# First channel product of a spectral mixer by Strassen's scheme, with its sums on VectorE

## The chip, the cores and the metric

The kernel runs on one core of one Trainium2 chip. The core has TensorE (PE in the profile; PEld is its weight load), VectorE (DVE), ScalarE (ACT), GpSimd (POOL) and the queue engine SP, each working through its own instructions in order, tied together by semaphores. The metric is the device time of one execution in microseconds (us); lower is better.

## The reference

```
X = rfft(x, axis=1)                                  # x: 8 x 3008 x 256
Yr = Xr @ w_r - Xi @ w_i + b_r ; Yi = Xr @ w_i + Xi @ w_r + b_i
Y = softshrink(Yr, 0.01) + 1j * softshrink(Yi, 0.01)
x = irfft(Y, n=3008, axis=1)                         # 8 x 3008 x 256
h = relu(x^T @ w_tok1) @ w_tok2                      # mixes the 3008 tokens
u = x + h^T
out = u + relu(u @ w_ch1) @ w_ch2                    # w_ch1: 256 x 1536, w_ch2: 1536 x 256
```

The last line is the channel stage, and it is the largest piece of work. `u @ w_ch1` is the first channel product; `relu(...) @ w_ch2` is the second.

## The kernel before

The 8 batches are handled in five units: `UNITS` is [0], [1], [2,3], [4,5], [6,7]. For each unit a spectral part (the `spectral` generator: Fourier transforms as matmuls, the complex product in `mix`, the inverse, and the token sums) comes first, and a channel part (`channel`) follows. The channel part of unit u and the spectral part of unit u+1 are interleaved by hand: at each `yield` of `channel` the main loop lets the spectral generator issue as many of its steps as a pace in `left_s` and `left_c` allows. The last unit's channel part has no spectral work beside it. From this program order the tile framework makes each engine's final order and adds the waits; each engine then runs its list strictly in that order.

Every product that feeds the output is made more precise by splitting both sides into a high and a low part in the type float32r: `mm3` issues three matmuls (high by high, high by low, low by high, L175 to L177) into one sum in PSUM.

The channel part walks over token chunks of up to 512 columns. A chunk of `u` (256 channels as 2 tiles of 128 rows) is made by `make_u` and split into `uh` and `ul` by `split_u`. There are 12 tiles of 128 hidden features. For each tile f:

- `first(f)`: 2 channel tiles by 3 passes, so 6 matmuls over the chunk's columns, into a PSUM bank `ph`.
- ACT writes `hh`, the rectified high part (L746), and DVE writes `hlo`, the rest (L747), both reading `ph`.
- `second(f)`: 6 matmuls of `hh` and `hlo` against `w2h` and `w2l` into `po`. It is issued two tiles later than `first(f)`, so that ACT and DVE have two tiles' time.

In the spectral part, `forward` makes `px` on PE, ACT copies it to `xf`, POOL adds its third plane (L424), and ACT and DVE split it into `xth` and `xtl`, which are the stationary sides of the 18 matmuls `pm` of `mix`. These tiles have two buffers, and `mix` of a step stands behind `forward` of the step after it. `tokens` adds all its products up in PSUM, in two banks `gp` that are held for the whole unit.

PSUM has 8 banks: 4 go round as `bank(...)`, two hold `po`, two hold `gp`.

## Time and profile before

| | |
|---|---|
| median of 3 runs | 2456.27 us (2453.36 to 2458.68) |
| the profiled execution | 2458.71 us, of which the span from the first to the last instruction is 2456.7 us |
| PE busy | 2423.6 us (99%), 12748 matmuls |
| PEld (weight loads, beside PE) | 2108.6 us (86%) |
| DVE busy | 1107.5 us (45%) |
| ACT busy | 873.3 us (36%) |
| POOL busy | 305.1 us (12%) |
| mean granted TensorE clock | 0.996 |

A matmul's duration in the profile covers its way through the array, and matmuls overlap: what one costs the queue is the distance from its start to the next one's start, called its pitch here. Idle time of an engine is put down to what ended it.

### The profile page before, as it was taken

What the parts mean: (1) busy time and instruction counts of PE and PEld (TensorE: products, weight loads), DVE (VectorE), ACT (ScalarE), POOL (GpSimd) and SP (SyncE); (2) the same over time, 40 slices, a digit from 0 to 9 for tenths busy, and PEclk for the clock granted to TensorE, in tenths of its full rate; (3) what the DMA queues carried; (4) which work ended last, traced back from release to release, by engine and by line L of the source; (5) the groups of instructions that cost most, each with busy time, mean ns of one, the idle gap of its engine ahead of it and who ended that gap; (6) DMA issues with size and microseconds to landing.
All of it is one profiled execution on the core that took longest, in us unless ns stands there. A gap on an engine that the chain in (4) does not pass through costs nothing.

```text
span 2456.7 us, 31566 instructions
## 1 busy us (share of the span) xinstructions
PE 2423.6 (99%) x12748; PEld 2108.6 (86%) x12748; DVE 1107.5 (45%) x1773; ACT 873.3 (36%) x1583; POOL 305.1 (12%) x259
## 2 busy tenths in 40 slices
PE   6999999999999999999999999999999999999999
PEld 5878999988888888888888898888888888888887
DVE  6975665454544444434344354434334333232332
ACT  4764444443334343333333343333333222222222
POOL 0000222222222111111111111111111000000000
PEclk8999999999999999999999999999999999999999
DMA  9775334552233462222222263222321112112110
GB/s 269 238 244 152 95 112 141 156 174 90 84 98 111 114 179 84 65 72 88 89 76 69 94 176 105 80 87 80 101 66 38 63 56 63 49 58 80 37 55 18
DMA packets 148946, 252.15 MB, mean 103 GB/s; under 512 B 11009, under 2 KB 101089, under 8 KB 148801
## 3 DMA queue, kind: packets, MB, share of 16 engines
q1 hardware_dynamic: 122289, 199.80, 27.2%
q10 hardware_dynamic: 26512, 50.34, 6.5%
q8 instruction: 100, 1.64, 0.3%
q14 instruction: 45, 0.37, 0.0%
HBM read 162.68 MB, written 87.43 MB: 102 GB/s over the span
## 4 chain that ended last, share of the span: by engine, by line
PE 93%; DMA 4%; DVE 1%; ACT 1%; SPq 0%; issue 0%; POOL 0%; DVEq 0%; ACTq 0%
PE ph L175 10%; PE ph L176 10%; PE po L175 10%; PE po L177 10%; PE po L176 10%; PE ph L177 10%; PE pu L708 4%; PE px L421 3%; PE pm L177 2%; PE pm L175 2%; PE pm L176 2%; PE pu L175 2%; PE pu L176 2%; PE pu L177 2%; PE gp L175 2%; PE gp L177 2%
## 5 line engine op out<-in xcount | busy, mean ns | idle before, releaser
L747 DVE SCALAR_TENSOR_TENSOR hlo<-ph,hh 128x512 fp32r<-128x512 f32 (+4 forms) x588 | 391.6, 667 | 646.0 <-ACT hh L746 643.0
L746 ACT ACTIVATE hh<-ph 128x512 fp32r<-128x512 f32 (+4 forms) x588 | 340.5, 580 | 815.8 <-PE ph L177 812.9
L175 PE MATMUL ph<-uh,w 128*128 128x512 f32 (+4 forms) x1176 | 456.0, 388 | 0.4 <-DVE hlo L747 0.3
L176 PE MATMUL ph<-ul,w 128*128 128x512 f32 (+4 forms) x1176 | 449.6, 382 | 0.3 <-DVE ul L717 0.3
L177 PE MATMUL ph<-uh,w 128*128 128x512 f32 (+4 forms) x1176 | 448.8, 382 | 0.0
L175 PE MATMUL po<-hh,w2h 128*128 128x512 f32 (+4 forms) x1176 | 448.7, 382 | 0.0
L176 PE MATMUL po<-hlo,w2h 128*128 128x512 f32 (+4 forms) x1176 | 448.1, 381 | 0.0
L177 PE MATMUL po<-hh,w2l 128*128 128x512 f32 (+4 forms) x1176 | 448.0, 381 | 0.0
L177 PEld LDWEIGHTS ph<-uh,w 128*128 128x128 f32 x1176 | 221.1, 188 | 39.4
L175 PEld LDWEIGHTS po<-hh,w2h 128*128 128x128 f32 x1176 | 221.1, 188 | 38.7
L176 PEld LDWEIGHTS po<-hlo,w2h 128*128 128x128 f32 x1176 | 221.0, 188 | 38.7 <-DVE hlo L747 0.2
L177 PEld LDWEIGHTS po<-hh,w2l 128*128 128x128 f32 x1176 | 220.9, 188 | 38.4
L175 PEld LDWEIGHTS ph<-uh,w 128*128 128x128 f32 x1176 | 221.5, 188 | 35.8 <-DVE hlo L747 1.4
L176 PEld LDWEIGHTS ph<-ul,w 128*128 128x128 f32 x1176 | 221.6, 188 | 34.6 <-DVE ul L717 0.7
L137 DVE TENSOR_TENSOR xtl<-xf,xth 128x768 fp32r<-128x768 f32 x84 | 80.5, 958 | 193.7 <-ACT xth L134 193.5
L715 ACT COPY uf<-pu 128x470 f32<-128x470 f32 (+23 forms) x188 | 62.6, 375 | 233.0 <-PE pu L708 233.0
L175 PE MATMUL pm<-wmh,xth 128*128 128x256 f32 x504 | 144.5, 287 | 0.1
L137 POOL TENSOR_TENSOR yl<-z,yh 128x512 fp32r<-128x512 f32 x72 | 92.7, 1288 | 413.2 <-ACT yh L134 413.2
L177 PE MATMUL pm<-wmh,xtl 128*128 128x256 f32 x504 | 142.5, 283 | 0.4 <-DVE xtl L137 0.3
L176 PE MATMUL pm<-wml,xth 128*128 128x256 f32 x504 | 142.4, 283 | 0.0
L708 PEld LDWEIGHTS pu<-g,b 96*128 96x128 f32 x1024 | 130.8, 191 | 3.4
L424 POOL TENSOR_TENSOR xf<-xf 128x256 f32<-128x256 f32 x84 | 69.7, 830 | 499.8 <-ACT xf L423 499.4
(124 smaller groups left out, 3213.5 us busy)
## 6 DMA issues: line engine op xcount, KB each, us to landing
wt<-wt_d SPq DMA_DIRECT2D x28, 940.0 KB, 5.5
x<-in_x SPq DMA_DIRECT2D x39, 480.0 KB, 4.3
a<-a_d SPq DMA_DIRECT2D x36, 512.0 KB, 3.9
b_d<-bt ACTq DMA_DIRECT2D x36, 512.0 KB, 3.3
out<-o SPq DMA_DIRECT2D x34, 512.0 KB, 2.8
a_d<-a ACTq DMA_DIRECT2D x36, 480.0 KB, 3.3
wt<-wt_d SPq DMA_DIRECT2D x21, 752.0 KB, 5.1
b<-b_d SPq DMA_DIRECT2D x32, 480.0 KB, 6.2
```

The lines of the kernel that those rows point to most:

```text
L137: lo_eng.tensor_tensor(out=lo, in0=src, in1=hi.bitcast(F32), op=ALU.subtract)
L175: PE.matmul(out, lhsT=wh, rhs=xh, start=start, stop=False)
L176: PE.matmul(out, lhsT=wh, rhs=xl, start=False, stop=False)
L177: PE.matmul(out, lhsT=wl, rhs=xh, start=False, stop=stop)
L421: PE.matmul(pt[:, o:o + 128], lhsT=x, rhs=f2cols(2 * kp + ab), start=True, stop=True)
L424: (V if plain else G).tensor_tensor(out=xf[:, 0], in0=xf[:, 1], in1=xf[:, 2], op=ALU.add)
L708: PE.matmul(pt[:, s * TOKS:(s + 1) * TOKS], lhsT=b2[:, s, cs], rhs=g2[:, 0 if s0 + s == 0 else 1], start=False, stop=s == k - 1)
L715: S.copy(out=ufs[m][:, ct, lo - at:hi - at], in_=pt[:, lo - c0:hi - c0])
L746: S.activation(out=hh, in_=pt, func=AF.Relu)
L747: V.scalar_tensor_tensor(out=hlo, in0=pt, scalar=0.0, in1=hh.bitcast(F32), op0=ALU.max, op1=ALU.subtract)
```

## The change

The first channel product is regrouped. A chunk's columns are cut into two halves of h = cw/2, the 256 channels into two tiles (already so), and the 12 feature tiles into 6 pairs. Per pair this is a 2 by 2 by 2 block product, which Strassen's scheme (in Winograd's form) makes with 7 block products in place of 8:

- `split_w1` makes from `w_ch1` four sums of blocks per pair (DVE) and stores 7 blocks, each split into high and low.
- `split_u(n, part)` makes four sums of blocks of the chunk (DVE) and splits 7 blocks `b11, b21, t1, t3, t2, t4, b22` (ACT high, DVE low). In the built program these are tiles named `u2_...` (two blocks each) and `u1_...` (`b22`).
- `pair(p)` makes the 7 products, each as 3 matmuls over h columns, into three PSUM banks `s1, s2, s3` (named `ph`), and adds them up: one copy on ACT (`cu`), three additions of h columns and two of cw columns on DVE.
- `features` takes such a sum of cw columns, written by DVE to SBUF (`hf`), rectifies it twice on ACT (once into `hh`, once in place), and subtracts on POOL: `hlo = hf - hh`. Before, ACT rectified once out of PSUM and DVE made `hlo` out of PSUM. The feature tile that comes from `s3` is called t1 in `pair`, the one from `s2` t0.
- `second` no longer issues its 6 matmuls; it puts them in a list `todo`, and `fill(k)` issues k of them at four places of the next pair.

`tokens` adds up in SBUF (`ga`): two matmul groups per step go to a bank and DVE adds them. The two PSUM banks so freed make the round 6 banks long. `hh` and `hlo` have 2 buffers in place of 3. The spectral tiles `xf, xth, xtl, wt, et` have one buffer in place of two, the output tile `o` has one in place of three, the loads of `w_d` and `e` go one step ahead in place of two, and `mix` of a step now stands ahead of `forward` of the next one. The chunks are cut anew: 48 (33 of 512 columns, 14 of 480, one of 448) in place of 49.

```diff
-    ps = ctx.enter_context(tc.tile_pool(name="ps", bufs=4, space=bass.MemoryType.PSUM))
+    ps = ctx.enter_context(tc.tile_pool(name="ps", bufs=6, space=bass.MemoryType.PSUM))
...
-        wt = wk.tile([128, 2, 2, DT], F32R, name="wt")
+        wt = wk.tile([128, 2, 2, DT], F32R, name="wt", bufs=1)
         split(wt[:, 0], wt[:, 1], wf, S, eng)
         return wt
 
     def split_e(ef, eng):
-        et = wk.tile([128, 2, 2, 128], F32R, name="et")
+        et = wk.tile([128, 2, 2, 128], F32R, name="et", bufs=1)
         split(et[:, 0], et[:, 1], ef, S, eng)
...
-    def split_w1(q, t, f):
-        cols = slice(q * 512, (q + 1) * 512)
-        split(wc["w1"][:, 0][:, t, cols], wc["w1"][:, 1][:, t, cols], f, S, V)
+    def split_w1(q, ws):
+        v0, v1 = (w.rearrange("p (r f c) -> p r f c", r=2, f=2) for w in ws)
+        sm = wk.tile([128, 4, 2, 128], F32, tag="o", name="ws", bufs=1)
+        V.tensor_tensor(out=sm[:, 0], in0=v0[:, :, 1], in1=v1[:, :, 1], op=ALU.add)
+        V.tensor_tensor(out=sm[:, 1], in0=sm[:, 0], in1=v0[:, :, 0], op=ALU.subtract)
+        V.tensor_tensor(out=sm[:, 2], in0=v0[:, :, 0], in1=v0[:, :, 1], op=ALU.subtract)
+        V.tensor_tensor(out=sm[:, 3], in0=v1[:, :, 0], in1=sm[:, 1], op=ALU.subtract)
+        d = wc["w1"][:, 2 * q:2 * q + 2]
+        split(d[:, :, 0, 0], d[:, :, 0, 1], v0[:, :, 0], S, V)
+        split(d[:, :, 1:3, 0], d[:, :, 1:3, 1], v1, S, V)
+        for k in range(4):
+            split(d[:, :, 3 + k, 0], d[:, :, 3 + k, 1], sm[:, k], S, V)
...
-            xh = wk.tile([128, 3, 2, 128], F32R, name="xth", bufs=2)
-            xl = wk.tile([128, 3, 2, 128], F32R, name="xtl", bufs=2)
+            xh = wk.tile([128, 3, 2, 128], F32R, name="xth", bufs=1)
+            xl = wk.tile([128, 3, 2, 128], F32R, name="xtl", bufs=1)
...
             if kp == 0:
-                acc.append(ps1.tile([128, 2, 512], F32, name="gp"))
-            gp = acc[0]
-            for i in range(2):
-                for jt in range(2):
-                    js = slice(jt * 128, (jt + 1) * 128)
-                    start, stop = kp == 0 and i == 0, kp == KP - 1 and i == 1
+                acc.append(ps1.tile([128, 2, 512], F32, tag="po", name="gp") if plain else wc["wk2"].tile([128, 2, 512], F32, name="ga", bufs=1))
+            ga = acc[0]
+            for jt in range(2):
+                js = slice(jt * 128, (jt + 1) * 128)
+                pt = ga[:, jt] if plain else bank("gp")
+                for i in range(2):
                     if plain:
-                        PE.matmul(gp[:, jt, :w], lhsT=wt[:, i, js], rhs=y[:, i], start=start, stop=stop)
+                        PE.matmul(pt[:, :w], lhsT=wt[:, i, js], rhs=y[:, i], start=kp == 0 and i == 0, stop=kp == KP - 1 and i == 1)
                     else:
-                        mm3(gp[:, jt, :w], wt[:, 0, i, js], wt[:, 1, i, js], rows(y, 0, i), rows(y, 1, i), start, stop)
+                        mm3(pt[:, :w], wt[:, 0, i, js], wt[:, 1, i, js], rows(y, 0, i), rows(y, 1, i), i == 0, i == 1)
+                if not plain:
+                    if kp == 0:
+                        V.tensor_copy(out=ga[:, jt, :w], in_=pt[:, :w])
+                    else:
+                        V.tensor_tensor(out=ga[:, jt, :w], in0=pt[:, :w], in1=ga[:, jt, :w], op=ALU.add)
...
-        for kp in range(2):
-            ws[kp] = load_w(w_d, kp), load_e(kp)
+        ws[0] = load_w(w_d, 0), load_e(0)
         lag = 4 if nb == 1 else 3
         for n in range(len(steps) + lag):
-            if n < len(steps):
-                kp, b = steps[n]
-                if b == 0 and kp + 1 < KP:
-                    a2s[kp + 1] = p.load_a(kp + 1)
-                xts[n] = p.forward(kp, b, a2s[kp])
-                yield 0.9
             m = n - 1
             if 0 <= m < len(steps):
                 kp, b = steps[m]
@@ -524,6 +531,12 @@
                         ys[kp] = hl([128, 2, 2, C], "yh"), hl([128, 2, 2, C], "yl")
                 p.mix(xts.pop(m), ys[kp][0][:, :, b], ys[kp][1][:, :, b])
                 yield 2.15
+            if n < len(steps):
+                kp, b = steps[n]
+                if b == 0 and kp + 1 < KP:
+                    a2s[kp + 1] = p.load_a(kp + 1)
+                xts[n] = p.forward(kp, b, a2s[kp])
+                yield 0.9
...
-            wc["w1"] = const.tile([128, 2, 2, DF], F32R, tag="w1", name="w1")
...
-        widths = [k * TOKS for k in sizes] if u == 0 else [total % CW] + [CW] * (total // CW)
+        short = -total % CW
+        widths = [CW - short] + [CW] * (total // CW) if u == 0 else [480] * (short // 32) + [CW] * ((total + short) // CW - short // 32)
...
+    def split_u(n, part):
+        h = chunks[n][2] // 2
+        if part == 0:
+            uf = ufs.pop(n)
+            sm = t4([128, 2, 2, CW // 2], "us")
+            us[n] = uf, {}, sm
+        uf, blocks, sm = us[n]
+        sums, more = sm[:, 0, :, :h], sm[:, 1, :, :h]
+        def block(names, src):
+            t = wc["wk2"].tile([128, 2, len(names), CW // 2], F32R, name=f"u{len(names)}", bufs={1: 1, 2: 4}[len(names)])
+            split(t[:, 0, :, :h], t[:, 1, :, :h], src, S, V)
+            for i, k in enumerate(names):
+                blocks[k] = t[:, 0, i, :h], t[:, 1, i, :h]
+        if part == 0:
+            V.tensor_tensor(out=sums, in0=uf[:, :, h:2 * h], in1=uf[:, 0, :2 * h].rearrange("p (i c) -> p i c", i=2), op=ALU.subtract)
+            V.tensor_tensor(out=more[:, 0], in0=uf[:, 1, h:2 * h], in1=sums[:, 0], op=ALU.subtract)
+            V.tensor_tensor(out=more[:, 1], in0=uf[:, 1, :h], in1=more[:, 0], op=ALU.subtract)
+            block(("b11", "b21"), uf[:, :, :h])
+        else:
+            block(("t1", "t3"), sums)
+            block(("t2", "t4"), more)
+            block(("b22",), uf[:, 1:, h:2 * h])
+    todo = []
+    def fill(k):
+        for _ in range(min(k, len(todo))):
+            todo.pop(0)()
     def channel(n):
         u, at, cw = chunks[n]
...
+        h = cw // 2
+        uf, blocks, _ = us.pop(n)
         after = chunks[n + 1] if n + 1 < len(chunks) else None
...
+        po = []
+        def product(out, p, a, b):
+            hi, lo = blocks[b]
+            mm3(out, wc["w1"][:, p, a, 0], wc["w1"][:, p, a, 1], hi, lo, True, True)
+        def add(out, x, y):
+            V.tensor_tensor(out=out, in0=x, in1=y, op=ALU.add)
+        def features(x, y):
+            hh, hlo, raw = (wc["wk2"].tile([128, CW], t, name=k)[:, :cw] for k, t in (("hh", F32R), ("hlo", F32R), ("hf", F32)))
+            add(raw.rearrange("p (i c) -> p i c", i=2), x, y)
+            S.activation(out=hh, in_=raw, func=AF.Relu)
+            S.activation(out=raw, in_=raw, func=AF.Relu)
+            G.tensor_tensor(out=hlo, in0=raw, in1=hh.bitcast(F32), op=ALU.subtract)
+            return hh, hlo
+        def second(f, t, first, last):
+            hh, hlo = t
+            w = (wc["w2h"], hh), (wc["w2h"], hlo), (wc["w2l"], hh)
             for ct in range(2):
...
+                for i, (m, x) in enumerate(w):
+                    def one(ct=ct, i=i, m=m, x=x):
+                        if first and ct == 0 and i == 0:
+                            po.append(ps1.tile([128, 2, 512], F32, tag="po", name="po"))
+                        PE.matmul(po[0][:, ct, :cw], lhsT=m[:, f, ct * 128:(ct + 1) * 128], rhs=x, start=first and i == 0, stop=last and i == 2)
+                    todo.append(one)
+            if last:
+                todo.append(store)
...
+        def halves(name):
+            return bank(name).rearrange("p (i c) -> p i c", i=2)[:, :, :h]
+        def pair(p):
+            s1, s2, s3 = (halves("ph") for _ in range(3))
+            u = wc["wk2"].tile([128, 2, CW // 2], F32, name="cu")[:, :, :h]
+            u3 = wc["wk2"].tile([128, CW // 2], F32, name="c3")[:, :h]
+            product(s1[:, 0], p, 0, "b11")
+            S.copy(out=u[:, 0], in_=s1[:, 0])
+            product(s1[:, 1], p, 4, "t2")
+            add(u[:, 1], s1[:, 1], u[:, 0])
+            fill(3)
+            yield 1.4
+            product(s2[:, 0], p, 1, "b21")
+            product(s1[:, 0], p, 5, "t3")
+            add(u3, s1[:, 0], u[:, 1])
+            fill(3)
+            yield 1.4
+            product(s3[:, 0], p, 2, "t4")
+            product(s3[:, 1], p, 3, "t1")
+            t1 = features(s3, u3.rearrange("p (o c) -> p o c", o=1).to_broadcast([128, 2, h]))
+            add(u[:, 1], s3[:, 1], u[:, 1])
+            fill(3)
+            yield 1.4
+            product(s2[:, 1], p, 6, "b22")
+            t0 = features(s2, u)
+            fill(4)
+            second(2 * p + 1, t1, p == 0, False)
+            second(2 * p, t0, False, p == NF // 2 - 1)
+            yield 1.04
+        def beside(f):
...
+        for p in range(NF // 2):
+            yield from beside(2 * p)
+            for i, c in enumerate(pair(p)):
+                yield c * cw / CW
+                if i == 1:
+                    yield from beside(2 * p + 1)
+        if after:
+            split_u(n + 1, 1)
```

What the order looks like on PE in the last unit, before: after a tile's six `ph` matmuls come the six `po` matmuls of an earlier tile, and the wait for `hlo` is on DVE.

```order
L177 MATMUL po<-hh,w2l 128x512
L175 MATMUL ph<-uh,w_336 128x512
L176 MATMUL ph<-ul,w_336 128x512
L177 MATMUL ph<-uh,w_336 128x512
...
L175 MATMUL po<-hh,w2h 128x512 [waits Activation_49]
L176 MATMUL po<-hlo,w2h 128x512 [waits DVE_49]
```

And now, in the same unit, from the last product into `s3` (`t1`, the tile u_26431) to the first use of the `hlo` made from it; u_26437 is `b22`, u_26372 holds `b11` and `b21` of the next pair, and the full stretch between the first three rows and the last is 3 `po`, 3 `b22`, 3 `po`, 3 `b11`, 1 `po`, 3 `b21`:

```order
L175 MATMUL ph<-u_26431,w_336 128x256
L176 MATMUL ph<-u_26431,w_336 128x256
L177 MATMUL ph<-u_26431,w_336 128x256
L798 MATMUL po<-hh,w2h 128x512
L798 MATMUL po<-hlo,w2h 128x512 [waits Pool_49]
...
L177 MATMUL ph<-u_26437,w_336 128x256
...
L798 MATMUL po<-hh,w2h 128x512 [waits Activation_49]
L175 MATMUL ph<-u_26372,w_336 128x256 [waits PE_49]
...
L798 MATMUL po<-hlo,w2h 128x512 [waits Pool_49]
L798 MATMUL po<-hh,w2l 128x512
```

The matmul that reads `hlo` now waits for POOL. On ACT, in the same place, one pair reads as follows: the two instructions for t1 come first, then the first one for t0, the copy out of `s1` of the next pair, and the second one for t0.

```order
L785 ACTIVATE hh_26152<-hf_26154 128x512 [waits DVE_49]
L786 ACTIVATE hf_26154<-hf_26154 128x512 [waits Activation_49]
L785 ACTIVATE hh_26166<-hf_26168 128x512 [waits DVE_49,PE_49]
L823 COPY cu_26179<-ph_26176 128x256 [waits PE_49]
L786 ACTIVATE hf_26168<-hf_26168 128x512 [waits Activation_49]
```

POOL issues its subtraction behind the second of each. In the spectral part, between a `px` group and the `pm` matmuls that read its split, PE had 67 rows in this place before, among them the whole `pm` of another step:

```order
L421 MATMUL px_10396<-f2_71,a2_9889 128x128 x3
L175 MATMUL po_9996<-hh_10314,w2h_1249 128x512 [waits Activation_49]
...
L175 MATMUL pm1_10422<-wmh_75,xth_10212 128x256 [waits PE_49]
...
L175 MATMUL pm1_10529<-wmh_75,xth_10404 128x256
L176 MATMUL pm1_10529<-wml_76,xth_10404 128x256
L177 MATMUL pm1_10529<-wmh_75,xtl_10405 128x256
```

Now there are 18 rows between, and they end with a wait for ACT and one for DVE:

```order
L429 MATMUL px_14033<-f2_70,a2_13341 128x128 x3
L175 MATMUL ph_14018<-u2_13568,w1_336 128x256 [waits DVE_49]
...
L798 MATMUL po_13752<-hlo_13981,w2h_1288 128x512 [waits Pool_49]
L798 MATMUL po_13752<-hh_13980,w2l_1289 128x512
L175 MATMUL pm1_14072<-wmh_74,xth_14041 128x256 [waits PE_49,Activation_49]
L176 MATMUL pm1_14072<-wml_75,xth_14041 128x256
L177 MATMUL pm1_14072<-wmh_74,xtl_14042 128x256 [waits DVE_49]
```

152 lines of the change are left out of this document (60 added, 92 removed).

## The prediction

> **What bounds the kernel now.** I read the engines' busy times first, then who waited for whom on PE, then the windows by stage.
>
> ```profile
> PE 2423.6 (99%) x12748; PEld 2108.6 (86%) x12748; DVE 1107.5 (45%) x1773; ACT 873.3 (36%) x1583; POOL 305.1 (12%) x259
> ```
> ```profile
> PE p L249 <- DVE sd L224: 9.6, 4, 6.2
> ...
> PE pm L177 <- DVE xtl L137: 0.3, 1, 0.3
> ...
> PE ph L175 <- DVE hlo L747: 0.3, 1, 0.3
> ```
> ```profile
> 0.00:100.00 100.00, 79.58 (x353) 63.95 (x354) 78.27 (x176) 58.60 (x105) 0.20 (x4) 0.91 0.88 258
> 100.00:200.00 100.00, 95.04 (x504) 76.09 (x503) 75.97 (x152) 59.46 (x120) 2.70 (x2) 1.00 0.70 217
> 800.00:1200.00 400.00, 400.00 (x2106) 347.95 (x2105) 170.91 (x247) 138.55 (x246) 55.14 (x48) 1.00 0.34 101
> 1930.00:2430.00 500.00, 500.00 (x2412) 427.23 (x2411) 152.50 (x209) 115.25 (x219) 2.57 (x2) 1.00 0.17 53
> ```
> (The second fence gives total wait, times, longest in us; in the third, after the stretch and its length, come the busy times of PE, PEld, DVE, ACT, POOL with counts, then the clock.) PE is the bound. After the first 200 us it never lacks work; waits for `hlo` and `xtl` cost it 0.3 us each in the whole run. So the time is PE's matmuls at their pitch, and two things can change it: fewer columns to stream, and new waits on PE.
>
> **What the seven products save.** From PE's timeline:
>
> ```profile
> 2050.46 0.39 PE L175 MATMUL po<-hh,w2h 128*128 128x512 f32 x1
> ...
> 2053.18 0.39 PE L175 MATMUL po<-hh,w2h 128*128 128x512 f32 x1
> ```
> ```profile
> 1516.78 0.28 PE L175 MATMUL pm<-wmh,xth 128*128 128x256 f32 x1
> ...
> 1518.94 0.40 PE L175 MATMUL ph<-uh,w 128*128 128x512 f32 x1
> ```
>
> Twelve matmuls of 512 columns lie between the first two rows: 2.72/12 = 0.2267 us each. Eighteen of 256 lie between the other two: 2.16/18 = 0.120, each with its own weights, so the weight loads hide at that pitch too. Twice 0.120 is 0.0133 more than 0.2267, so a matmul costs 0.417 ns a column and 0.0133 us besides. Per pair of feature tiles at 512 columns the first product was 12 x 0.2267 = 2.72 us and becomes 21 x 0.120 = 2.52, with 2.72 for the second product unchanged: 5.24 for 5.44. Over everything: 8 x 3008 = 24064 columns, 72 - 63 = 9 fewer streamings of them (126 over half the columns are 63) are 90.2 us; 6 x 21 x 48 = 6048 matmuls for 3528 (1176 x 3) cost 33.5 back, and the 49th chunk's 72 `po` matmuls save 1. **-57.7 us.**
>
> The Trainium skill (TensorE: Matmul & The Clock Gate, Back-to-back issue gap) gives 262 cycles for 256 columns and 518 for 512, 2.5 ns besides the columns. By that the estimate would be -84 us. The trace has 13.3 ns, and is used.
>
> **What the new chain costs.** `hlo` was made in two steps out of PSUM. Now it is a DVE addition, two ACT passes one behind the other, and a POOL subtraction. Nearest rows by shape and source (mean ns last before the bar):
>
> ```profile
> L446 DVE TENSOR_TENSOR z<-pm,bias 128x512 f32<-128x512 f32 x96 | 65.5, 683 | 25.6 <-PE pm L177 25.5
> L447 DVE TENSOR_TENSOR z<-pm,z 128x256 f32<-128x256 f32 x96 | 40.4, 421 | 13.8 <-PE pm L177 11.2 <-DVE z L446 0.5
> ```
> ```profile
> L134 ACT CAST yh<-z 128x512 fp32r<-128x512 f32 x72 | 44.8, 622 | 42.7 <-DVE z L455 42.6
> L451 ACT ACTIVATE z<-z,sc 128x512 f32<-128x512 f32 x12 | 8.7, 724 | 0.4 <-ACT z L450 0.2
> ```
> ```profile
> 2431.55 0.39 PE L177 MATMUL ph<-uh,w 128*128 128x512 f32 x1
> ...
> 2431.97 0.60 ACT L746 ACTIVATE hh<-ph 128x512 fp32r<-128x512 f32 x1 [2.12 <-PE ph L177]
> ...
> 2432.61 0.69 DVE L747 SCALAR_TENSOR_TENSOR hlo<-ph,hh 128x512 fp32r<-128x512 f32 x1 [2.03 <-ACT hh L746]
> ```
> ```profile
> 605.24 0.62 ACT L134 CAST yh<-z 128x512 fp32r<-128x512 f32 x1 [1.72 <-DVE z L455]
> 605.94 1.29 POOL L137 TENSOR_TENSOR yl<-z,yh 128x512 fp32r<-128x512 f32 x1 [5.83 <-ACT yh L134]
> 606.39 0.69 DVE L747 SCALAR_TENSOR_TENSOR hlo<-ph,hh 128x512 fp32r<-128x512 f32 x1 [0.59 <-ACT hh L746]
> ```
>
> The last matmul into a bank starts at 2431.55, gives PE free at +0.227, and its reader starts at 2431.97: 0.19 us. Then DVE 0.68, ACT 0.62 twice (0.72 at most, the row with a bias tile), POOL 1.29 (the same subtraction; a DVE operation that reads PSUM beside it does not lengthen it), and handovers of 0.04, 0.04, 0.08 and, taken like them, 0.05 to PE, less some 0.1 by which ACT overlaps two instructions: **3.5 us** at 512 columns, 3.3 at 480. Bounds: 3.4 and 3.8.
>
> The cover is what the order puts on PE between the last t1 matmul and its `hlo`: in the quoted stretch 6 `po`, 3 `b22`, 3 `b11`, 1 `po`, 3 `b21` = 7 x 0.2267 + 9 x 0.120 = 2.67 us. PE's list is strict, so it stands still for 3.5 - 2.67 = 0.83 us, and behind it stand all later products. A pair then takes 5.24 + 0.83 = 6.07 us, 0.63 more than before.
>
> I did this subtraction for each of the 288 pairs of the new order, with the pitches above (0.10 for matmuls of under 200 columns, from the eight `px` between 1524.40 and 1525.21 further below) and 3.5, 3.3 and 3.1 us for the three widths:
>
> | unit | pairs | short of cover | sum of shortfalls, us |
> |---|---|---|---|
> | [0] | 36 | 15 | 12.3 |
> | [1] | 36 | 18 | 14.3 |
> | [2,3] | 72 | 33 | 24.7 |
> | [4,5] | 72 | 33 | 25.1 |
> | [6,7] | 72 | 54 | 46.5 |
>
> The last unit has no spectral work beside it; only `make_u` covers some pairs. **+47 us** there, **+76** in the others. The t0 tile has 4 us or more almost everywhere: nothing, except at the very end of the kernel, +2.
>
> In the other units the chain shares its engines with spectral work. Outside the features a DVE, ACT and POOL instruction lasts 0.4 to 1.3 us, and the engines were busy 43%, 35% and 14% in 800:1200; five handovers that each find one in progress every third or fourth time make the chain some 0.3 us longer. By the same subtraction the sum in these units grows from 76 to 109: **+33**. Bounds 0 and, for 1.0 us, +125.
>
> **Other new waits.** Between `px` and the matmuls that read its split:
>
> ```profile
> 1524.40 1.05 PE L421 MATMUL px<-f,a 128*128 128x128 f32 x8
> 1525.21 0.48 PE L175 MATMUL ph<-uh,w 128*128 128x512 f32 x1
> ...
> 1525.50 0.59 ACT L423 COPY xf<-px 128x512 f32<-128x512 f32 x1 [1.66 <-PE px L421]
> ```
> ```profile
> 1527.87 0.96 DVE L137 TENSOR_TENSOR xtl<-xf,xth 128x768 fp32r<-128x768 f32 x1 [3.31 <-ACT xth L134]
> ```
>
> PE is done issuing `px` at 1525.21, `xtl` is ready at 1528.83: 3.62 us, hidden before by the whole `mix` of another step. With one buffer and the new order, 44 of the 84 steps leave less; the shortfalls add up to some 40 us. The second product into `s1` waits for ACT's copy out of the same bank (0.62 us, shortfalls 7 us in all), and the third for DVE's addition (0.65, shortfalls 20). These stalls and those for `hlo` lie in each other's covers, so I take half of 67: **+34**, bounds 0 and 67.
>
> Costed at nothing: `ga` additions (46 of 0.68 us and less) and the 0.68 us `split_u` sums lie beside PE, at the DVE load above, and are in the 0.3 us; PSUM's longer round only helps. At the start DVE gains 3 x 4 sums of 0.42 us and smaller splits, about 9 us, while PE is only 80 to 95% busy: **+8**, bounds 0 and 15.
>
> Sum: -58 + 47 + 76 + 33 + 34 + 2 + 8 = +142 us on 2458.7, the profiled execution; the median lies 2.4 lower: 2456.3 + 142 = 2598. Forecast **2598 us**.
>
> **Rivals.**
> *The chain fits its cover.* It decides if DVE, ACT and POOL together take under 2.2 to 2.7 us, the common covers at 480 and 512. Then no wait is left: -58 + 8 = 2406. For it: neighbouring instructions of one engine overlap. Against it: four dependent steps from rows, POOL alone 1.29.
> *Only the last unit waits.* Spectral matmuls fall into the stretches elsewhere: -58 + 47 + 10 = 2455, the same as before. Against it: 99 of 216 pairs there are short by the count.
> *The engines' queues decide.* An instruction that waits at the head of ACT's, DVE's or POOL's list for a late PE blocks the chain behind it: 1 us more per chain, and the other waits in full, is -58 + 47 + 76 + 125 + 67 + 10 = +267, 2723. For it: each list mixes both kinds of work. Against it: the spectral work comes in lumps some pairs apart.
> *The clock falls.* The stretch 0:100, with PE at 80%, was granted 0.91. At 0.95 in the mean, 2300 us of matmuls cost 120 us more: 2715. Against it: 100:200 had 1.00 at 95%. The Trainium skill (TensorE: Matmul & The Clock Gate, on PSUM cycling) tells of a kernel whose frequent small idles made the clock swing between half and full; no run here shows stalls of 0.8 us yet.
>
> **How the numbers follow.** Differences under 0.2% (5 us) cannot be told from none here. Forecast 0.68, queues 0.15, clock 0.06, only the last unit 0.05, fits 0.06. Faster: the fit and a small part of "last unit" = 0.07; same 0.03; slower 0.90. Range: low end 2500, with the queueing and other waits at nothing and part of the 76 covered (-58 + 47 + 55 = +44); high end 2700, most of the queue case.
>
> **What would show it.** Waits of `po` for POOL `hlo` at about 0.8 us, some 150 or more of them, adding to over 100 us; PE's busy share down to 92 to 95% with a last unit of about 6.1 us a pair; POOL's `hlo` at 1.29; waits of `pm` for `xtl`; a clock still near 1.0. The forecast is wrong if those waits are few, or if ACT rectifies out of SBUF in much under 0.6 us.

## The result, and the profile after

The changed kernel takes 2919.39 us (median of 4 runs, 2917.05 to 2923.75) against 2455.76 us (4 runs, 2453.36 to 2458.68): ratio 1.189, 95% interval 1.187 to 1.191. The direction was forecast, the size was not: +464 us where +142 was expected and +244 was the upper end. The profiled execution has a span of 2922.0 us, 465.3 more than before.

The page's first part and the waits of PE in the changed kernel (total us, times, longest):

```profile
PE 2580.4 (88%) x15196; PEld 2221.5 (76%) x15196; DVE 1658.9 (57%) x2982; ACT 1385.6 (47%) x2647; POOL 1038.8 (36%) x835
```
```profile
PE po L798 <- POOL hlo L787: 156.4, 174, 2.8
PE ph L175 <- DVE cu L780: 46.3, 68, 2.9
PE pm L175 <- ACT xth L134: 26.4, 27, 2.9
PE ph L175 <- ACT cu L823: 26.1, 26, 2.1
PE po L798 <- DVE o L808: 24.0, 17, 3.5
PE po L798 <- ACT hh L785: 15.5, 22, 2.3
...
PE pm L177 <- DVE xtl L137: 4.5, 10, 0.5
```

PE was at 99% and waited for nearly nothing. Now it waits for five other things beside `hlo`, and the clock, 0.996 before, is 0.962. All rows of this view add to 333.7 us in 362 waits; before they added to 28.2 us in 20, nearly all at the start.

Windows cut at the units' first `ph` (stretch, its length, busy time of PE, PEld, DVE, ACT, POOL, clock), with units [2,3] and [6,7] here, first before the change and then after it:

```profile
836.00:1424.00 588.00, 588.00 (x3075) 509.97 (x3074) 248.11 (x365) 199.46 (x355) 86.47 (x73) 1.00 0.31 94
...
2011.00:2457.00 446.00, 441.34 (x2122) 376.82 (x2120) 133.72 (x180) 99.49 (x190) 0.00 (x0) 1.00 0.17 51
```
```profile
991.00:1694.00 703.00, 628.06 (x3720) 541.51 (x3720) 379.74 (x666) 326.77 (x620) 271.48 (x218) 0.97 0.27 79
...
2397.00:2922.00 525.00, 462.02 (x2749) 392.87 (x2747) 242.06 (x453) 224.76 (x451) 185.46 (x146) 1.00 0.13 41
```

By the same cuts the five units took 301, 370, 588, 588 and 446 us before and take 378, 443, 703, 703 and 525 now: +77, +73, +115, +115, +79, and +5 ahead of the first. The last unit, which has no spectral work and a clock of 1.00, loses as much as unit [0].

The pieces of the feature chain last nearly what was assumed (mean ns behind the comma):

```profile
L787 POOL TENSOR_TENSOR hlo<-hf,hh 128x512 fp32r<-128x512 f32 x396 | 524.8, 1328 | 776.8 <-ACT hf L786 661.4 <-DVE hf L780 43.3 <-PE ph L177 20.6
```
```profile
L780 DVE TENSOR_TENSOR hf<-ph,c 128x512 f32<-128x512 f32 x198 | 136.5, 690 | 98.0 <-PE ph L177 86.6 <-POOL hlo L787 8.2
```

**What one wait costs.** PE's timeline in the last unit:

```profile
2480.26 0.38 PE L798 MATMUL po<-hh,w2h 128*128 128x480 f32 x1
2480.49 0.38 PE L798 MATMUL po<-hlo,w2h 128*128 128x480 f32 x1
...
2481.26 0.38 PE L798 MATMUL po<-hh,w2h 128*128 128x480 f32 x1
2482.80 0.49 PE L798 MATMUL po<-hlo,w2h 128*128 128x480 f32 x1 [1.15 <-POOL hlo L787]
2483.12 0.38 PE L798 MATMUL po<-hh,w2l 128*128 128x480 f32 x1
2483.34 0.28 PE L175 MATMUL ph<-u,w 128*128 128x240 f32 x1
```

Without a wait, the next matmul starts 0.22 us later (2480.26 to 2480.49, 2483.12 to 2483.34). The waiting one starts 1.54 us after its forerunner, 1.32 over that pitch, though the view writes 1.15 idle: it counts from the modelled end of a matmul, which lies 0.17 us past its pitch. And the first matmul after the wait needs 0.32 to the next start, 0.10 more than the others. The weight loads (PEld) at that place show why:

```profile
2482.79 0.19 PEld L798 LDWEIGHTS po<-hlo,w2h 128*128 128x128 f32 x1 [1.45 <-POOL hlo L787]
2482.90 0.19 PEld L798 LDWEIGHTS po<-hh,w2l 128*128 128x128 f32 x1
2483.12 0.19 PEld L175 LDWEIGHTS ph<-u,w 128*128 128x128 f32 x1
```

The load for the matmul at 2483.12 starts at 2482.90, ahead of it; the load for the one that waited starts only with it, at 2482.79. It is so everywhere: the loads of all 362 waiting matmuls start within 0.03 us of them, while 13362 of the other 14834 loads start over 0.1 us ahead of theirs. So a wait costs some 0.27 us beyond its idle time. For 362 - 20 = 342 waits more than before that is 92 us.

**Where the clock went.** A window ahead of a low clock, and the one after it, with PE's rows:

```profile
1696.30:1699.71 3.41, 1.31 (x7) 0.83 (x6) 3.41 (x4) 1.89 (x3) 3.41 (x3) 1.00 0.00 0
1699.71:1706.54 6.83, 4.92 (x14) 3.98 (x15) 3.99 (x6) 1.42 (x3) 2.20 (x2) 0.50 0.69 178
```
```profile
1696.38 0.28 PE L177 MATMUL ph<-u,w 128*128 128x240 f32 x1
1698.50 0.50 PE L798 MATMUL po<-hlo,w2h 128*128 128x512 f32 x1 [1.84 <-POOL hlo L787]
...
1701.62 0.57 PE L175 MATMUL ph<-u,w 128*128 128x240 f32 x1 [2.16 <-DVE cu L780]
```

PE was busy 1.31 of 3.41 us at full clock, and then was granted half. The clock's records come in steps of 3.41 us. They sum to 224 us at half clock (22 before); a stretch of it is called low here. I summed PE's idle time over the pitch in the 3.41 us ahead of each of the 34 low stretches after 300 us: it is 1.95 to 3.17 us in all of them. Of the 690 steps there at full clock with another one at full clock behind them, 4 reach 1.95 us and 90% have under 1.3. In the last unit, where PE waits for `hlo` mostly 0.8 to 1.2 us and seldom twice within 6.5, there is one low stretch of 3.4 us. So the clock did not fall by itself; it fell behind clusters of waits. The Trainium skill (TensorE: Matmul & The Clock Gate, Why this matters for your kernels) asks for no idle gap over about 3 us; by that rule gaps of 1.8 and 2.2 us would do no harm. The trace has half clock behind gaps of 1.8 us, if they add to 2 us or so in one such step.

**The sum, by the profiles:** -58 for the pitch (each span less all that PE's starts show over the pitch: 2282 now, 2340 before), +305.5 for the waits as the view has them (333.7 - 28.2), +92 for what each costs besides, +93 for the clock (what lies over the pitch in low stretches, 105 now and 11 before; half of 202 us would be 101): 433 of 465. Two things make up the rest. The view lists no idle time under 0.15 us: by PE's starts, 1114 more matmuls at full clock have their successor start over 0.03 us late, by 111 us in all, where before it was 628 and 64 us, so +47. And some 11 us of the listed waits lie in low stretches and are counted twice.

### The profile page after: what moved, and what is told of

It is laid out like the page before. It is cut to its first block, busy times and chain, and to the rows that moved or that the text cites. A ratio compares the mean times of both kernels' runs of the same rounds, so it can differ in the third digit from the quotient of the medians.

```text
span 2922.0 us, 40831 instructions
## 1 busy us (share of the span) xinstructions
PE 2580.4 (88%) x15196; PEld 2221.5 (76%) x15196; DVE 1658.9 (57%) x2982; ACT 1385.6 (47%) x2647; POOL 1038.8 (36%) x835
## 3 DMA queue, kind: packets, MB, share of 16 engines
q8 instruction: 119, 1.95, 0.3%
## 4 chain that ended last, share of the span: by engine, by line
PE 59%; DVE 14%; POOL 10%; ACT 8%; issue 6%; DMA 2%; SPq 0%; POOLq 0%; DVEq 0%; ACTq 0%
PE po L798 17%; POOL hlo L787 7%; PE ph L175 7%; PE ph L177 5%; PE ph L176 5%; PE pu L726 4%; DVE hf L780 4%; PE pm L175 2%; PE pm L177 2%; PE pm L176 2%; ACT hf L786 2%; ACT hh L785 2%; PE px L429 2%; PE pu L175 2%; PE pu L176 2%
## 5 line engine op out<-in xcount | busy, mean ns | idle before, releaser
L787 POOL TENSOR_TENSOR hlo<-hf,hh 128x512 fp32r<-128x512 f32 (+2 forms) x576 | 743.4, 1297 | 1243.0 <-ACT hf L786 1056.8
L175 PE MATMUL ph<-u,w 128*128 128x256 f32 (+2 forms) x2016 | 612.0, 305 | 73.9 <-DVE cu L780 46.3
L785 ACT ACTIVATE hh<-hf 128x512 fp32r<-128x512 f32 (+2 forms) x576 | 358.5, 622 | 643.9 <-DVE hf L780 626.3
L798 PE MATMUL po<-hlo,w2h 128*128 128x512 f32 (+2 forms) x1152 | 477.8, 415 | 156.7 <-POOL hlo L787 156.4
L176 PE MATMUL ph<-u,w 128*128 128x256 f32 (+2 forms) x2016 | 572.2, 285 | 0.5 <-DVE u L137 0.5
L177 PE MATMUL ph<-u,w 128*128 128x256 f32 (+2 forms) x2016 | 569.4, 285 | 0.0
L175 PEld LDWEIGHTS ph<-u,w 128*128 128x128 f32 x2016 | 390.6, 194 | 187.0 <-DVE cu L780 91.9
L798 PE MATMUL po<-hh,w2h 128*128 128x512 f32 (+2 forms) x1152 | 463.5, 402 | 40.1 <-DVE o L808 24.0
L798 PE MATMUL po<-hh,w2l 128*128 128x512 f32 (+2 forms) x1152 | 455.5, 395 | 0.0
L176 PEld LDWEIGHTS ph<-u,w 128*128 128x128 f32 x2016 | 392.1, 195 | 35.9 <-DVE u L137 0.9
L780 DVE TENSOR_TENSOR cu<-ph,cu 128x256 f32<-128x256 f32 (+2 forms) x576 | 236.8, 411 | 314.8 <-PE ph L177 311.4
L177 PEld LDWEIGHTS ph<-u,w 128*128 128x128 f32 x2016 | 391.0, 195 | 1.3
L786 ACT ACTIVATE hf<-hf 128x512 f32<-128x512 f32 (+2 forms) x576 | 357.8, 622 | 12.1
L780 DVE TENSOR_TENSOR hf<-ph,c 128x512 f32<-128x512 f32 (+2 forms) x288 | 195.2, 678 | 144.5 <-PE ph L177 132.1
L780 DVE TENSOR_TENSOR hf<-ph,cu 128x512 f32<-128x512 f32 (+2 forms) x288 | 194.8, 676 | 49.9 <-PE ph L177 29.2
```

The costliest lines, as they stand in the source:

```text
L175: PE.matmul(out, lhsT=wh, rhs=xh, start=start, stop=False)
L176: PE.matmul(out, lhsT=wh, rhs=xl, start=False, stop=False)
L177: PE.matmul(out, lhsT=wl, rhs=xh, start=False, stop=stop)
L780: V.tensor_tensor(out=out, in0=x, in1=y, op=ALU.add)
L785: S.activation(out=hh, in_=raw, func=AF.Relu)
L786: S.activation(out=raw, in_=raw, func=AF.Relu)
```

## The experiments

Theory after the result: PE stands still for several late results in turn, the feature chain first, then the additions out of shared PSUM banks, then the spectral split; and the clock follows these stops. Rivals: the clock falls by itself and is the main cause; the engines can't deliver at this pace whatever the order; the spectral part is at fault. Where no other kernel is named, a diff is against the changed kernel. A ratio is to the kernel before on the same chip, which took 2455 to 2456 us there each time. The expectations count a wait from PE's starts, over the pitch, which is more than the view's idle time: "about 202 us" for `hlo` where the view has 156.

**e1, no wait for a feature.**

```diff
-            hh, hlo = t
+            hh, hlo = (x[:, :cw] for x in wc["fixed"])
```

> All products, block products, features and additions are as in the changed kernel, but the second channel product reads two fixed tiles in place of the features hh and hlo (its output is therefore not the reference's), so that no matmul waits for a feature. My theory now: the waits of po for hlo (about 202 us in the profile of the changed kernel), half of those for hh (25), the slow first matmul behind each such wait (about 50 of 79) and the half-clock windows that follow these waits (70 of 92) go together: 2919 - 202 - 25 - 50 - 70 = 2572, range 2530 to 2640, mean granted clock at 0.985 or more; the waits of ph for cu (112 us) stay and are what is left over the pitch. If the clock fell for another reason (more products in the same time, not the gaps), it stays at 0.96 to 0.97 and the time is 2640 or more. If the waits for cu take the place of those for hlo, the time stays above 2750 with the clock low.

2826.83 us, ratio 1.151 (1.150 to 1.153), clock 0.964. Only 93 us gone, a miss. The waits of PE:

```profile
PE ph L175 <- ACT cu L828: 109.4, 79, 5.0
PE ph L175 <- DVE cu L784: 69.6, 81, 4.6
PE pm L175 <- ACT xth L134: 39.6, 38, 3.3
```

`ph` waited 72 us for `cu`, now 179. The last rival of the expectation holds: with one reason for the stop removed, PE gets earlier to the next late thing.

**e2 and e3, a shorter chain.** e2 writes `V.tensor_tensor` for `G.tensor_tensor` in L787; e3 drops a pass too:

```diff
-            S.activation(out=raw, in_=raw, func=AF.Relu)
-            G.tensor_tensor(out=hlo, in0=raw, in1=hh.bitcast(F32), op=ALU.subtract)
+            V.scalar_tensor_tensor(out=hlo, in0=raw, scalar=0.0, in1=hh.bitcast(F32), op0=ALU.max, op1=ALU.subtract)
```

> One step of the feature chain moves: the subtraction that makes hlo is on VectorE, 0.69 us (as its addition hf) in place of 1.33 on GpSimd. If the length of the chain against its cover decides, each of the 174 waits shortens by up to 0.64 us, 0.6 on the mean, less what VectorE's queue adds: 2919 - 105 = 2815, range 2760 to 2860, clock only a little up. If VectorE's queue decides (240 us of work more on it, 1659 to 1900), the time stays at 2890 or more and the waits move from hlo to cu and o. If the clock decides by itself, 2890 or more with the clock at 0.96.

> The chain loses two pieces: the second pass of ScalarE (0.63 us) is left out, and hlo is made by one VectorE instruction, max(hf, 0) - hh, at 0.69 us in place of GpSimd's 1.33. The chain of 3.5 us becomes 2.2, under the cover of 2.67. Theory: nearly all of the hlo waits go (202 us), most of the slow first matmuls behind them (50), half of the half-clock time (45), and some of the waits for ScalarE's cu since ScalarE has 220 us less to do: 2610, range 2560 to 2700, clock 0.98 or more. Rival, VectorE's queue: its waits for cu and o grow by as much as the chain saves, 2800 or more. Rival, the clock by itself: 2680 or more at 0.96.

e2: 2788.2 us, 1.135 (1.134 to 1.137). e3: 2795.58 us, 1.138 (1.136 to 1.141). e2 is inside its range and gained more than 105; e3, with a still shorter chain, no more than e2, far from 2610 and close to its rival, VectorE's queue (2800). But that rival's waits are not what grew: in e3 `cu` waits for ScalarE, 80.0 us, more than for VectorE, 29.2. PE's waits in e2 and in e3:

```profile
PE ph L175 <- ACT cu L823: 58.6, 50, 4.4
PE ph L175 <- DVE cu L780: 44.2, 67, 2.9
PE po L798 <- DVE hlo L787: 40.5, 55, 2.3
```
```profile
PE ph L175 <- ACT cu L822: 80.0, 70, 2.8
PE pm L175 <- ACT xth L134: 30.1, 30, 2.8
PE ph L175 <- DVE cu L780: 29.2, 57, 1.7
...
PE po L797 <- DVE hlo L786: 15.3, 35, 1.3
```

The `hlo` waits fall from 156 to 40 and 15 as the chain shortens, and `ph` waits over 100 us for `cu` in both. The chain is a cause, and there is a second one right behind it.

**e4, the same instructions with more work ahead of the readers.** (The `yield` lines, whose paces change with the order and add up to the same, are left out.)

```diff
             add(u[:, 1], s1[:, 1], u[:, 0])
-            fill(3)
             product(s2[:, 0], p, 1, "b21")
+            product(s3[:, 0], p, 2, "t4")
+            fill(4)
             product(s1[:, 0], p, 5, "t3")
             add(u3, s1[:, 0], u[:, 1])
-            fill(3)
-            product(s3[:, 0], p, 2, "t4")
             product(s3[:, 1], p, 3, "t1")
+            fill(4)
             t1 = features(...)
...
-            fill(3)
             product(s2[:, 1], p, 6, "b22")
+            fill(5)
             t0 = features(s2, u)
-            fill(4)
```

> Same instructions and same arithmetic, other order on TensorE: b11, t2, b21, t4, 4 matmuls of the second product, t3, t1, 4 more, b22, 5 more, in place of 3 behind each pair of block products. The features of s3 are needed later: between product t1 and the first matmul that reads hlo lie 4 + 1.6 products' worth, 0.91 + 0.36 + 1.13 + 1.45 + 0.23 = 4.1 us, against 2.67 before, and between t2 and t3, which waits for the VectorE addition of s1, 1.63 us instead of 1.04. Theory (cover against chain): hlo waits under 30 us, ph waits for cu under 70, slow first matmuls halved, clock 0.98 or more: 2919 - 180 - 45 - 45 - 60 = 2590, range 2520 to 2680. Rival, the engines' queues (VectorE, ScalarE and GpSimd can't deliver at that pace): the waits move to later places and the time stays above 2780. Rival, the clock by itself: 2680 or more at 0.96.

2806.4 us, 1.143 (1.141 to 1.145): a miss on the time. Its waits:

```profile
PE ph L175 <- ACT cu L823: 152.6, 113, 5.8
PE po L798 <- POOL hlo L787: 37.0, 48, 3.3
```

The cover works (`hlo` 156 to 37), but product t2 now follows b11 closely and waits for ACT's copy of b11, which reads the other half of the same bank.

**e6, that wait removed by one line's place; e7, with e3's short chain.**

```diff
             product(s1[:, 0], p, 0, "b11")
-            S.copy(out=u[:, 0], in_=s1[:, 0])
             product(s1[:, 1], p, 4, "t2")
+            S.copy(out=u[:, 0], in_=s1[:, 0])
```

> The later order of e4, and in it ScalarE's copy of b11 is written behind product t2 in place of ahead of it, so that t2, which goes into the other half of the same bank, has no copy to wait for. Theory: in e4 the waits of ph for cu on ScalarE (152.6 us, 113 times) are t2's wait for that copy, and they go; t3's wait for VectorE's addition grows by at most the 0.36 us by which the copy comes later, and has 1.6 us of matmuls ahead of it. 2806 - 110 = 2700, range 2650 to 2760, clock up to 0.975. Rival, the queues: the copy is late because ScalarE's list stands behind hh and hf, whatever waits for it, and the wait moves to t3 and hlo: 2780 or more.

> As e6, and the second pass of ScalarE left out, hlo = max(hf, 0) - hh on VectorE as in e3. The chain for the features is 2.2 us against a cover of 4.1, so no hlo wait has a reason of its own; ScalarE has 220 us less and VectorE 290 us more to do. Theory: 2700 - 60 = 2640, range 2580 to 2700, clock 0.975 or more. Rival, VectorE's queue with 1930 us of work in 2700: the waits for cu on VectorE are 100 us or more and the time is not under e6's.

e6: 2700.16 us, 1.101 (1.099 to 1.103), clock 0.974; e7: 2616.09 us, 1.066 (1.064 to 1.068), clock 0.976. Both as the theory had it, e6 to the microsecond by luck. In e6 the row for `cu` on ACT has left the first places:

```profile
PE ph L175 <- DVE cu L780: 68.3, 49, 3.6
PE po L798 <- POOL hlo L787: 60.4, 67, 3.3
PE pm L175 <- ACT xth L134: 31.9, 30, 3.4
```

106 us came from a copy that is written one product later. That the engines can't deliver at this pace is thereby out as the main cause: their work is the same in e4 and e6.

**e10, the two shared banks alone**, in the changed kernel's own order: e6's swap, and

```diff
-            s1, s2, s3 = (halves("ph") for _ in range(3))
+            s1, s2, s3, s4 = (halves("ph") for _ in range(4))
...
-            product(s1[:, 0], p, 5, "t3")
-            add(u3, s1[:, 0], u[:, 1])
+            product(s4[:, 0], p, 5, "t3")
+            add(u3, s4[:, 0], u[:, 1])
```

> The changed kernel in its own order, with the two waits for a shared bank taken away alone: ScalarE's copy written behind t2, and t3 in a bank of its own. The feature chain stays at 3.5 us with its old cover. In the profile of the changed kernel these waits are 72 us (46 for VectorE, 26 for ScalarE), 112 over the pitch. If they add to the others, 2919 - 100 = 2820. If they lie in each other's cover with the waits for hlo (what e1 showed the other way round), hlo grows by about half of that: 2870, range 2830 to 2910. I take the second.

2777.38 us, 1.131 (1.129 to 1.133), clock 0.976: 142 us gone, more than either case. Its waits:

```profile
PE po L798 <- POOL hlo L787: 146.6, 154, 2.2
PE pm L175 <- ACT xth L134: 31.9, 35, 2.7
PE po L798 <- DVE o L808: 30.5, 19, 5.7
```

`hlo` waits did not grow (156 to 147) when the 72 us for the banks went, so those gave `hlo` no cover, and the two kinds of stops add. The other way round it is not so: in e1, without the `hlo` waits, those for `cu` grew by 107 us. All waits fell by 54 us and 93 in number (25 us by 0.27 each), and the time at half clock from 224 to 137 us (43): 122 of the 142.

**e5, b1, b2: the spectral part.** e5 puts the order in `spectral` back in the changed kernel; b1 has the spectral part of the change without the block products; b2 is b1 with the order put back:

```diff
-            m = n - 1
-            ... mix of step n-1
             if n < len(steps):
                 ... forward of step n
+            m = n - 1
+            ... mix of step n-1
```

> The changed kernel with the order of the spectral program put back: the forward transform of step n is written ahead of the mix of step n-1, as before the change. The single buffers for the spectral tiles stay. If the order makes the waits of pm (26 us for xth, 4.5 for xtl, 53 over the pitch with the slow first matmuls), they go and the time falls by about 50, to 2870. If the single buffer makes them, the forward's split now has to wait for the mix that stands behind it on TensorE, at the head of ScalarE's and VectorE's lists, and the time stays or rises: 2900 to 2980. I take the second.

> The kernel before the change with the spectral part of the change alone: single buffers for xf, xth, xtl, wt and et, mix written ahead of the next forward, the split of wt and et as late as in the change, and the token sums in SBUF by VectorE. The first channel product is the old one in eight block products. My price for these edits was 20 of 40 us for the waits of pm plus VectorE's additions at nothing. Theory: the old order leaves less for TensorE to do between px and pm only in some steps, 2456 + 40 = 2496, range 2465 to 2530, with waits of pm for xth and xtl of 20 to 50 us in the profile. Rival, they are harmless without the new chain, since the engines are less loaded: 2450 to 2465. Rival, they are most of the loss: 2600 or more.

> As b1 (the kernel before the change with the spectral part alone, 2503.7 us), with the order put back, so that single buffers, the later splits and the token sums by VectorE remain. If the order is what costs: 2460 to 2475, pm waits under 8 us. If the single buffer costs, since a split now waits for the mix that is next on TensorE: 2490 to 2510. By e5 I take the first.

e5: 2873.96 us, 1.171 (1.169 to 1.173); b1: 2503.7 us, 1.020 (1.019 to 1.022); b2: 2457.96 us, 1.001 (1.000 to 1.002). The order costs 46 us by itself and 45 in the changed kernel; single buffers, later splits and token sums on VectorE cost 2 us together. My pick for e5 was wrong. In b1 PE waits for what the prediction had named:

```profile
PE pm L175 <- ACT xth L134: 18.7, 22, 2.4
PE pm L177 <- DVE xtl L137: 9.5, 21, 0.7
```

**e8 and e9, on top of e7:** t3's own bank as in e10, then the spectral order.

> As e7, and product t3 goes into a PSUM bank of its own (four of the six banks for a pair in place of three), so that it waits neither for ScalarE's copy nor for VectorE's addition out of s1. Theory: the waits of ph for cu on VectorE in e7 (64.4 us, 60 times, 0.32 each in the last unit) are t3's wait for its bank and nearly all go, with the slow first matmul behind each: 2616 - 50 = 2566, range 2535 to 2600; the last unit takes 425 to 432 us in place of 451. Rival, VectorE's queue: the addition itself is late, its next readers are the features, and the waits move to hh and hlo or to the bank's next round: 2600 or more, last unit 440 or more.

> As e8, with the spectral program's order put back (the forward of step n ahead of the mix of step n-1), single buffers kept. e5 gave 45 us for that in the changed kernel, e7 still has 30 us of pm over the pitch. Theory, the order makes the waits for xth: 25 us under e8, 2540, range 2515 to 2575, waits of pm under 10 us. Rival, the gain of e5 lay in the stalls of the feature chain and not in pm: within 8 us of e8.

e8: 2576.3 us, 1.050 (1.048 to 1.051); e9: 2537.2 us, 1.033 (1.032 to 1.035), clock 0.983; both inside their ranges. The waits for `cu` on VectorE fell from 64 to 10 us. The last unit came to 441 us, missing 425 to 432; `po` waits there for `o`, 6.5 us in e9. But that is under the 446 us of the kernel before, so there the seven products pay. e9's first part of the page, and its units [2,3] and [6,7]:

```profile
PE 2420.5 (95%) x15196; PEld 2174.7 (86%) x15196; DVE 1931.0 (76%) x3558; ACT 1073.0 (42%) x2071; POOL 301.6 (12%) x259
```
```profile
896.00:1499.00 603.00, 587.22 (x3725) 529.94 (x3724) 454.92 (x810) 248.61 (x476) 87.09 (x74) 0.99 0.31 92
...
2099.00:2540.00 441.00, 429.90 (x2751) 391.63 (x2749) 319.80 (x599) 148.69 (x305) 0.00 (x0) 1.00 0.16 48
```

With the same number of matmuls as the changed kernel, the clock is back to 0.99 and 1.00 in these units. The clock by itself is out as a cause.

**e11, e12, e13: what e9 still loses.** e11 gives t0's `hlo` back to ACT's second pass and POOL, e12 also makes the two `po` banks tiles of their own, e13 is e9 with those tiles and e1's fixed tiles.

```diff
+            if near:      # t1 only
                 V.scalar_tensor_tensor(out=hlo, in0=raw, scalar=0.0, ...)
+            else:
+                S.activation(out=raw, in_=raw, func=AF.Relu)
+                G.tensor_tensor(out=hlo, in0=raw, in1=hh.bitcast(F32), op=ALU.subtract)
```

> As e9, and of the two feature tiles of a pair the later-needed one (t0) makes hlo the way of the changed kernel, by ScalarE's second pass and GpSimd, while t1 keeps the short way on VectorE. VectorE has 140 us less to do (1931 to about 1790). Theory: what is left in e9 of waits for hh, hlo, o and cu (55 us, and the slow first matmuls behind them) comes from VectorE's list, above all in the first unit: 2537 - 18 = 2519, range 2500 to 2535. Rival: the two engines lengthen each other's additions and ScalarE's second pass holds up xth and cu: 2545 or more.

> As e11, and the second product's two banks are tiles of their own, each added and freed by itself at a chunk's end, so that the next chunk's first po waits for one addition of 0.69 us in place of one of two banks. In e9 po waits 18.2 us for o, 16 times, with a slow first matmul behind each. Theory: 15 us under e11, 2504, range 2485 to 2525. Rival: the addition is late by what stands ahead of it on VectorE, not by its length: within 5 us of e11.

> As e9 with the two po tiles of e12, and the second product reads two fixed tiles in place of the features, as in e1 (its output is not the reference's). This gives what is left of the loss when no feature can be waited for. The pitch of e9's matmuls alone is 2283 us; before the change 116 us came on top of the pitch, which no edit here touched. Theory, nearly all else that e9 lost were waits that hang on features and o: 2283 + 116 + 30 for the token sums, the loaded start and the clock = 2430, range 2400 to 2465. Rival, the spectral part and the start lose as much by themselves now: 2490 or more.

e11: 2599.64 us, 1.058 (1.057 to 1.060), 62 us worse than e9, a miss in sign. e12: 2588.72 us, 1.054 (1.053 to 1.056), 11 under e11, between its two cases. e13: 2516.75 us, 1.025 (1.023 to 1.026), its rival. For e11, the additions `cu` by shape, first in e9 and then in e11 (idle time of VectorE ahead of them and what ended it):

```profile
L780 DVE TENSOR_TENSOR cu<-ph,cu 128x256 f32<-128x256 f32 x396 | 164.5, 416 | 23.0 <-ACT cu L823 22.0
```
```profile
L780 DVE TENSOR_TENSOR cu<-ph,cu 128x256 f32<-128x256 f32 x396 | 164.7, 416 | 103.7 <-ACT cu L827 102.5
```

VectorE waits 102.5 us for ACT's copy of b11 in place of 22.0. The second pass for t0 stands ahead of that copy in ACT's list, and the copy begins the next pair's chain. That t0 itself is needed late does not help: what counts is who stands behind it. This reading is from the trace; no run moved the copy ahead.

e13 says that features and `o` are worth 20 us of e9's 81. By units it takes 345, 380, 594, 593 and 436 us where the kernel before took 301, 370, 588, 588 and 446: 44 us are lost in unit [0]. A stretch there, in e13 and before:

```profile
170.00:270.00 100.00, 73.24 (x399) 63.92 (x398) 83.52 (x175) 46.71 (x90) 0.00 (x0) 0.80 0.49 152
```
```profile
165.00:270.00 105.00, 104.10 (x577) 93.15 (x576) 73.73 (x140) 51.62 (x93) 7.13 (x7) 1.00 0.49 148
```

VectorE is 84% busy in that stretch with weights, spectral sums and block sums, PE 73% busy, and the clock at 0.80. PE's longest waits in it are three of 4.1 to 4.9 us for `wt`, the token weights, which ScalarE splits when VectorE has made `wide` (L155); before the change no wait in it is over 0.3 us. Which of VectorE's jobs sets it was not tried. No version here beats the kernel before.

## Why the prediction was wrong

| step of the prediction | predicted, us | by the profile after, us |
|---|---|---|
| seven products at their pitch | -57.7 | -58 |
| `hlo` stalls, last unit | +47 | +47.7, 51 waits |
| `hlo` stalls, other units, with queues | 76 + 33 | +108.7, 123 waits |
| second and third product into `s1` | half of 27 | +72.4, 94 waits |
| `px` to `xth`, `xtl` | half of 40 | +30.9, 37 waits |
| `hh` and `o` | 2 at the end | +39.5, 39 waits |
| ahead of the first unit | +8 | +5 |
| what a wait costs beside its idle time | 0 | +92 |
| clock | 0, a rival at 0.06 | +93 |

(The last unit's `hlo` waits are that view over 2397 to 2922: 47.7 us, 51 times.)

**What held.** The bound, the pitch with its 13.3 ns per matmul (12503 of the 15196 matmuls now start the next one within 0.03 us of it), and the kind of stall: the chain is longer than its cover, and in the last unit 51 pairs wait where 54 were counted as short. By the Trainium skill's figure (TensorE: Matmul & The Clock Gate, Back-to-back issue gap), which the prediction named and did not use, the pitch term was -84; by the trace it is -58.

**What agrees in part by luck.** The `hlo` rows. The chain was 0.2 us longer than forecast: in the last unit, from PE's being done to the start of the matmul that waits, 3.68 us (median) at 512 columns and 3.52 at 480, for 3.5 and 3.3. The view's idle time leaves out 0.17 us of each wait and hides that; counted over the pitch, as the prediction counts, the 51 waits are 56.5 us and not 47. And the 33 for queues was a guess with bounds 0 and 125.

**What failed first: "These stalls and those for `hlo` lie in each other's covers, so I take half of 67".** e10 shows that those for `s1` come on top of those for `hlo`. And the 27 us for `s1` were too few already: they assume that ACT's copy and VectorE's addition start when PE is done, but these stand in one list with the features' additions and passes, which wait for PE in their turn. Of the 288 copies, 208 come right behind a pass for the features on ACT. I had a term for such queues, 33 us, and put it on the `hlo` chain alone. For `hh` and `o` I had none: the single `o` and the `po` banks that are freed late were read in the diff and left at nothing. The spectral order, half of 40, costs 46 (b1 against b2).

**What failed next: a wait was priced too low.** 342 new waits at 0.27 us over their idle time are 92 us. Of each, 0.17 us is lateness that the view does not show, and which the shortfalls, counted over the pitch, should have held; 0.10 us is the slow matmul behind the wait, for which there was no term. The rows to see it were there, in PE's timeline before the change:

```profile
166.56 0.48 PE L176 MATMUL ph<-ul,w 128*128 128x470 f32 x1 [0.29 <-DVE ul L717]
166.88 0.38 PE L177 MATMUL ph<-uh,w 128*128 128x470 f32 x1
```

From 166.56 to 166.88 are 0.32 us for 470 columns, whose pitch is 0.21. I read only pitches in stretches without a wait.

**And the clock rival.** I gave it 0.06 "against: 100:200 had 1.00 at 95%". That is a mean over 100 us; what decides is PE's idle time within 3.4 us. The trace before the change shows it once: PE waits 0.32 us at 504 and 2.21 us at 507, and the only step at half clock after 300 us begins at 508. It is no rival at all but an addition to each case with many stalls, +93 here. The prediction cited a rule of the Trainium skill on frequent small idles (TensorE: Matmul & The Clock Gate, A second HAM failure mode: psum-queue depth-cycling) and found no stalls of 0.8 us to judge by. The trace agrees with that rule only where the waits cluster: single waits of about 1 us, mostly over 6.5 us apart, left the clock at 1.00 in the last unit; waits that added to about 2 us within 3.4 halved it.

The rival nearest to the result is "the engines' queues decide", 2723, with the right place and a price at under 60% of what came. "The chain fits" and "only the last unit waits" are out by the `hlo` row.

## What to carry to other kernels

When an in-order engine loses its cover, list everything that it will wait for, not the longest chain alone: removing one wait shows the next (e1, e4), stops of different kinds can add (e10), and each costs its idle time plus some 0.27 us here. Count PE's idle time per clock step of 3.4 us: about 2 us of it halved the clock of the work that followed. Two halves of a PSUM bank that different engines read are one resource to the waits, so write the products into a bank first and its readers after, or give each its own bank; the two together were worth 142 of 464 us here (e10).

## What the runs showed that I had not expected

- Half clock follows 3.41 us with about 2 us or more of idle PE, with no single gap over 3 us needed; when the waits had fallen from 333.7 to 114.0 us, the time at half clock had fallen from 224 us to 88 (e9).
- A matmul that waits for its moving side holds up its own weight load as well (all 362 here), and the next matmul starts 0.10 us later than the pitch.
- VectorE's subtraction with two SBUF inputs is longer beside GpSimd's. The same instruction in the changed kernel, and in e2, where GpSimd makes no `hlo`:

```profile
L137 DVE TENSOR_TENSOR u<-uf,u 128x256 fp32r<-128x256 f32 x33 | 28.6, 867 | 2.4 <-ACT u L134 2.3
```
```profile
L137 DVE TENSOR_TENSOR u<-uf,u 128x256 fp32r<-128x256 f32 x33 | 15.7, 476 | 0.0
```

  867 ns against 476 in the mean; single ones in the changed kernel last from 0.41 to 1.52 us. The Trainium skill (SBUF — State Buffer, SBUF: two separate sides) says that the two engines share a port pair under an exclusive lock, taken by a VectorE operation with two SBUF inputs against a GpSimd one that reads SBUF; the trace agrees.
